# Clustered attention and a SoLU layer on one core: v rows 72 elements apart, contiguous key tiles, and every engine's order written anew

## The chip, the cores and the metric

The kernel runs on one core of one Trainium2 chip. The metric is the device time of one execution in microseconds (us), the median of several runs. TensorE (PE), VectorE (DVE), ScalarE (ACT), GpSimd (POOL) and SyncE (SP, which issues the transfers) each take their own instructions in order and wait for one another by semaphores.

## What is computed

Four batches, eight heads, 768 tokens, heads of 64. Queries and keys are each assigned to one of 16 clusters, a query attends to keys of its own cluster, and the result passes through a layer of width 1024 with a softmax-gated unit and a normalisation:

```
q_assign = argmax(q_n @ c_n);  k_assign = argmax(k_n @ c_n)
scores   = where(q_assign == k_assign, (q @ k.T) / 8, -1e9)
attn     = softmax(scores) @ v                    # 4 x 8 x 768 x 64
x        = attn, heads side by side               # 3072 x 512
h        = x @ w_in                               # 3072 x 1024
u        = h * softmax(h)
out      = ((u - mean(u)) / sqrt(var(u) + 1e-6) * g_ln) @ w_out
```

## The kernel before

**Pairs.** The work is cut into 16 pairs of heads (4 batches with 4 pairs), and the pairs' results into 24 blocks of 128 tokens for the layer (f = 0 to 23). For each pair the loads bring q and k as fp32 (tile `raw`). In batch 0 tokens lie on partitions and TensorE turns them (L387); in batches 1 to 3 the load (`load`, L397) puts blocks of 32 tokens by 32 columns, and DVE's 32x32 stream transpose (`turn`, L408, output `xt`) turns each block in place. Then `xt` is cast into the bf16 tile `qk` (L434, L436; ACT in batch 0, L432), rows 0 to 63. Four small matmuls on `xt` give the cluster scores (L446, L451, `csc`); DVE turns them back (L460, `cst`), takes the maximum (L473), makes one-hot rows (L479, L485), turns these (L492, L495, `oht`), and they are placed as 16 or 32 more rows under the heads in `qk` by DVE, POOL or, in four cases, an SP transfer (L507, L513, L515). With them the score matmul adds a large constant where query and key share a cluster, and the exponential takes it away again, so that no mask is needed.

**Attention.** `scores` (L602) multiplies a tile of 128 keys (the weights) with 128, 256 or 384 queries into one of three PSUM banks `sps`; ACT's exponential (L608) writes `e`; `values` (L625) takes 128x128 of `e` as the weights and a row of v as the moving operand, 64 columns and one column of ones for the denominators, six matmuls for each block of 128 queries, into `ops`, of which there is one bank. `normalise` (L637, L650) divides into `x`. In batches 1 to 3 the keys of tile kt are `slice(kt, S, n_t)`, every sixth column of `qk` from kt on, to fit v, which is loaded with six neighbouring tokens on one partition (`load_v`, L528; cast by L533 to `v1`). In batch 0 the keys of a tile are already neighbours in `qk`.

**The layer.** For block f: an SP transpose `xT` (L680), two matmul groups h into two of three banks `hreg` (L711), the row maximum (L717, `nmax`), the exponential (L723, `e_sb`), the product u (L730), statistics (L741, L745), an SP transpose `uT` (L735), matmuls y with the centred w_out (L775, `yps`), the scale (L751 to L760 on POOL for alpha; L790 on ACT or L792 on DVE) and the store (L802).

**What sets the order.** Every piece of work is an operation with a name (`S12.1` for a bank of scores, `V12.0` for six value matmuls, `h5.0.1`, `xt1.2.1`, `ld1.2.1.2`, `li0`). `Weave.ORDER` (L28) holds for each of the five engines a text of kinds and repeats, as `S2 V h`; `queues` (L108) takes the operations of a kind in turn. `AWAY` says which operations leave their usual engine. An operation's needs become semaphore waits. A transfer of SP also waits until the earlier one that used its completion semaphore has landed, so that only some transfers are in flight. Idle matmuls (`wm`, `fl`, L820) run on TensorE in the first 10 us, where it has nothing else to do.

Of the kernel before, what the change touches and what calls it, by code (L numbers as in the profile page):

```python
# [10 lines left out]
F32 = mybir.dt.float32  # L11
BF16 = mybir.dt.bfloat16
# [10 lines left out]
class Weave:  # L23
# [3 lines left out]

    ORDER = {}  # L28
    ORDER["SP"] = """
        ld4 lv si ld4 lv lg ld4 lv2 ld4 lo2 ld4 lo ld3 lo ld3 li4 tx ld3 lv3 tx ld4 tu ld9 lv ld tu  # L30
        tx ld3 tu ld3 ou ld2 ou ld tu ld12 tu ld4 lv ld2 ou tx ld3 tu ou ld2 tx lv ld tu ld4 tx ld
        tu ou2 ld lv ld4 tu ld4 tu ld ou ld7 pl ou ld lv2 ld3 tu lv tx ou tu lv pl ld4 ou2 tx lv tu
        tx ou tu pl2 tu2 tx tu tx ou2 tx ou tu tx2 ou tu2 ou2 tu2 ou6
    """
    ORDER["POOL"] = """
        po z ca2 pl2 cv z bl pl2 ca z ca pl2 ca z2 ca3 cv ca cv ca pl3 sg ca cv2 pl3 ca2 gs pl ca cv
        ca wi ca pl2 wi3 bl ca pl2 cv at cv pl ca pl al bl at cv ca pl ca pl cv ca3 al at ca al ca
        at ca pl2 bl cv pl2 ca4 at ca2 al ca pl2 bl pl2 cv2 ca3 al at pl2 bl pl2 ca pl al ca3 at cv
        at pl ca pl2 ca2 pl al cv2 bl cv2 pl2 ca pl al pl at al at pl2 ca3 at al bl cv pl2 bl cv2
        ca3 pl5 al cv3 at al ca2 cv ca cv ca2 at ca2 pl ca al pl2 at2 pl3 at ca cv al at2 al2 at2 al  # L40
        at al3 at al2 at2 al2
    """
    ORDER["PE"] = """
        wm tp fl3 cp fl2 tp2 cl tp fl10 cl fl8 S3 tp2 S2 tp S cq S tp S2 tp2 S2 V3 S cl S tp2 V3 S gt S tp S
        tp S2 cl S2 V2 S V S2 tp S2 tp S2 V2 S V S2 cl S2 V2 S V2 S3 V S2 V2 S2 V S cl S3 su S2 V3 S
        V S3 V3 S2 V S su S2 V S V3 S3 me S3 V4 S3 cl S3 V4 S2 h S h S2 h S h S2 V3 S2 V h S h V S V
        S h S V S V S h S2 V3 S2 V h S2 h V2 S y3 S2 h3 S3 y V3 h V S2 V2 S cl S3 h2 S2 V3 S y2 S V
        h2 S V y2 S h S V h S2 h S y3 S2 y V3 h S3 cl V2 S V S y S2 y2 S3 V3 S y S2 V3 S2 cl S V S2
        V2 S h S2 V2 S V S h S2 V2 cl V2 S3 y2 S V S2 V y S2 y V2 S3 h2 S V h S h S2 V h S V S V y2
        S h V y2 S2 V S h3 S cl V S2 V2 S h V cl S3 h2 V y V S3 y2 V S h V3 S y S h S2 h2 S3 V2 y h  # L50
        S V S2 y V3 y S3 h3 y S3 V3 S h S V S V cl S V S h S cl V2 S3 y V2 S y S2 y V2 S3 h y V S3 V
        h V2 S3 cl S2 V2 S y3 S2 y S V3 S V S y S2 V S V3 S2 y2 S3 y V2 S2 h V2 S3 h3 S V S2 V y S V
        h2 V2 S y S2 y V y S h2 S3 cl h V S2 V3 S h V2 S3 h2 S y S2 V h S2 V y2 V4 S3 y h S2 h V h V
        S V S y2 S3 V3 h2 S2 h2 S2 y2 S V S h2 S V3 S2 h S h S2 V S y V2 S V y2 S2 h2 S2 h2 V2 S2 V2
        y S2 h V2 h V S2 h S V h S3 V2 h y S V y3 V h3 S2 y3 S2 y h2 V2 h y h y3 h V h V y4 h ptx h
        y4 h2 y3 h2 y ptu2 y6 ptu y ptu y5
    """
    ORDER["DVE"] = """
        cn cb xa ca tb mx oh ot pl2 tb mx oh ot xa3 bl cf cv xa zo xa2 tb ca mx oh gk N ot tb pl mx
        xa2 oh xa cv N ot tb pl N xt mx xt N oh ot tb pl2 ca N pl xt mx N sk oh N ot xt ce3 N tb ce5  # L60
        N hm mx N u oh ot bn N bn ag hm xt2 u N bn2 hm ag sc xt u N bn tb hm mx bn oh ag u xt bn ot
        xt N cv hm bn ag sc xt tb mx N u xt oh ot sc N bn2 xt ag xt tb N hm mx tb N oh ot u xt mx N
        bn oh bn xt hm ot ag N cv u bn2 xt hm tb mx u N tb oh mx hm ot bn2 oh ag u N sc ag hm bn ot
        u bn N xt2 ag xt2 hm tb N bl mx tb bn2 oh u N xt ag xt sc hm ot tb mx oh N bn sc N u bn N ag
        xt ot bn ca N mx sc oh hm u bn ag N xt hm bn2 bl tb u ot ag N hm mx bn2 u bn N oh ot hm bl2
        u ag N cv hm sc bn u N hm ag bn N bn u bn2 hm ag2 N bn u bn2 N ag hm bn u N ag hm bn2 u bn2
        hm sc u N ag2 bn tx hm bn sc u bn ag hm bn tu ag u2 bn2 ag sc
    """
    ORDER["ACT"] = """
        wa xa2 ca2 xa ca2 E12 xa2 E6 xa E58 ex E12 ex E8 ex E8 ex E3 sc E5 ca E2 ex E25 ex E9 sc E6  # L70
        ex E5 sc E2 ex E9 ex E8 ex E9 sc E6 ex E18 ex E21 ex E5 sc E3 ex E9 ex E7 sc E2 ex E7 ex E8
        ex E7 ex E6 sc E ex E2 sc E3 ex E2 sc ex sc ex sc ex tu sc tu2 sc2 oz
    """
    AWAY = {}
    AWAY.update(dict.fromkeys("""
# [35 lines left out]
    def queues(self):  # L111

        of = {}
        for i, o in enumerate(self.ops):
            of.setdefault((o["eng"], o["kind"]), []).append(i)
        queues = {}
        for e, text in self.ORDER.items():
            queues[e] = []
            for kind, n in re.findall(r"([A-Za-z]+)(\d*)", text):
                for _ in range(int(n or 1)):  # L120
                    queues[e].append(of[e, kind].pop(0))
        assert not any(of.values()), {k: len(v) for k, v in of.items() if v}
        return queues
# [46 lines left out]
def kernel(  # L170
# [42 lines left out]
    mo = ctx.enter_context(tc.tile_pool(name="mo", bufs=2))  # L213
# [32 lines left out]
    SRC = (q, k)  # L246
# [35 lines left out]
    for b in range(B):  # L282
        for p in range(n_pair):
            a, c = 2 * p, 2 * p + 1
# [112 lines left out]
    def load(b, p, i, c, eng):  # L397
        if (b, p, i) not in raws:
            raws[b, p, i] = ld.tile([P, n_j, NB], F32, name="raw")
        eng.dma_start(  # L400
            out=raws[b, p, i][c * NB:(c + 1) * NB],
            in_=SRC[i][b, 2 * p + c // 2, :, (c % 2) * NB:(c % 2 + 1) * NB]
            .rearrange("(j i) c -> i j c", i=NB))
# [174 lines left out]

    def keep_sums(e):
        src = hreg[:, 1, :]  # L580
        uses(nc.scalar.copy(w_sum[:], src) if e == "ACT" else
             nc.vector.tensor_copy(w_sum[:], src), 1)

    def mean_w_out():
        uses(nc.tensor.matmul(hreg[:, 2, :], g_mean[:], w_sum[:]), 1, 2)

    def centre_w_out(fc):
        uses(nc.vector.scalar_tensor_tensor(out=w_out_c[:, fc, :], in0=w_g[:, fc, :],
# [6 lines left out]
    def scores(n, k):  # L595
        u = UNITS[n]
        b = u["b"]
        sps_[n, k] = ps_s.tile([P, 512], F32, name="sps", tag="sps")
        for h, kt, s0, w, c0 in u["banks"][k]:
            r = used(b, h)  # L600
            keys = slice(kt * P, (kt + 1) * P) if by_token(b) else slice(kt, S, n_t)
            nc.tensor.matmul(sps_[n, k][:, c0:c0 + w], side(b, h // 2, 1, h % 2, keys)[r],  # L602
                             side(b, h // 2, 0, h % 2, slice(s0 * P, s0 * P + w))[r])

# [234 lines left out]
    nc.gpsimd.memset(v1[0][:, :, :, D:], 1.0)  # L839

    c_n = const.tile([P, 2, D], F32, name="c_n")
    c_nsq = const.tile([P, 1], F32, name="c_nsq")
# [58 lines left out]
    for idx, (b, p) in enumerate(pairs):  # L901
        first = first_of(b, p)
        if by_token(b):
            for hf, i in ((hf, i) for hf in range(2) for i in range(2)):
                if not halves_of(b, p):
                    i, hf = hf, i
                t = f"{b}.{p}.{i}"
# [6 lines left out]
                e = "ACT" if (b, p) == (0, 0) and i == hf else "DVE"  # L914
# [5 lines left out]
        for i in range(2):  # L920
            t = f"{b}.{p}.{i}"
# [30 lines left out]
            for hh in range(2):  # L952
                for hf in range(2) if halves_of(b, p) else (None,):
# [3 lines left out]
                    e = "ACT" if hf is not None and i == 1 else "POOL"  # L957
# [5 lines left out]
        t = f"{b}.{p}"  # L963
# [297 lines left out]
```

## Time and profile before

| what | value |
|---|---|
| median of 3 runs | 226.29 us (224.62 to 227.29) |
| span of the profiled execution | 223.1 us, 3.2 us less than the median |
| instructions in the profile | 6642 |
| busy share of the span | PE 96%, DVE 88%, ACT 86%, POOL 57% |
| first score matmul | at 9.52 us |
| read from HBM, written to it | 23.11 MB, 6.29 MB |

The profile is one execution, from the first instruction to the last; the runs' times also hold what lies around it. An engine's busy time is the union of its instructions, and a matmul's end in it is modelled: matmuls overlap in the pipeline, so what a stream of them costs is read from the distance of their starts, not from their mean duration. Some matmul records can be missing. A row of a group names the line, the engine, the operation, output <- inputs, shapes and count, then busy us, mean ns of one, and the idle time of the engine before them.

### The profile page before, as it was taken

The numbers are of one execution on the slowest core, as the hardware profiler recorded it, in microseconds if no ns is written. First come the engines' busy times: TensorE is split into PE (matmuls) and PEld (weight loads), VectorE is DVE, ScalarE is ACT, GpSimd is POOL, SyncE is SP. The second block draws the span as 40 slices with busy tenths as digits, with TensorE's granted clock in tenths as the row PEclk, the third lists the DMA queues.
The fourth block names the chain that finished last, engine by engine and source line by source line (L and its number), as shares of the span: only waits on it lengthen the run. The fifth ranks groups of instructions, "written<-read, shape, count | busy, mean of one in ns | idle before, by whom it ended". The sixth has DMA issues, their size and how long they took to land.

```text
span 223.1 us, 6642 instructions
## 1 busy us (share of the span) xinstructions
PE 214.7 (96%) x2422; PEld 149.8 (67%) x2454; DVE 197.0 (88%) x359; ACT 192.1 (86%) x372; POOL 127.0 (57%) x247
## 2 busy tenths in 40 slices
PE   7899999999999999999999999999999999999994
PEld 6576656677566777776577667787677777755452
DVE  3799898999999989999998999887999889888982
ACT  3779999999888999998889899999999998983363
POOL 3499842774793999547668543944796403022331
PEclk9999999999999999999999999999999999999999
DMA  6999888989999998899999879199940528385923
GB/s 151 333 299 183 240 171 240 341 203 200 166 180 180 207 156 152 190 174 205 149 268 152 175 147 240 67 207 220 223 59 9 98 51 140 79 156 148 177 80 141
DMA packets 125679, 38.80 MB, mean 174 GB/s; under 512 B 115016, under 2 KB 121168, under 8 KB 125648
## 3 DMA queue, kind: packets, MB, share of 16 engines
q1 hardware_dynamic: 123904, 37.87, 82.3%
q10 hardware_dynamic: 1744, 0.52, 1.0%
q8 instruction: 19, 0.31, 0.6%
q14 instruction: 12, 0.10, 0.1%
HBM read 23.11 MB, written 6.29 MB: 132 GB/s over the span
## 4 chain that ended last, share of the span: by engine, by line
PE 83%; ACT 5%; DVE 4%; issue 3%; DMA 3%; SPq 1%; ACTq 0%; DVEq 0%
PE sps L602 27%; PE hreg L711 17%; PE yps L775 17%; PE ops L625 14%; ACT e L608 5%; PE csc L451 4%; DMA raw<-in_q_dram 2%; PE hreg L387 1%; DVE u L730 1%; DMA raw<-in_k_dram 1%; PE hreg L575 1%; PE hreg L775 1%; PE csc L446 1%; DVE bs L741 1%; DVE xt L408 0%
## 5 line engine op out<-in xcount | busy, mean ns | idle before, releaser
L608 ACT ACTIVATE e<-sps 128x512 bf16<-128x512 f32 (+1 forms) x294 | 151.1, 599 | 12.2 <-PE sps L602 10.2
L602 PE MATMUL sps<-qk 80*128 80x256 bf16 (+5 forms) x636 | 94.0, 264 | 1.4 <-ACT e L608 0.5
L602 PEld LDWEIGHTS <-qk 80*128 80x128 bf16 (+1 forms) x636 | 60.1, 121 | 27.6 <-issue 9.0
L625 PEld LDWEIGHTS <-e 128*128 128x128 bf16 x1152 | 50.4, 97 | 12.4 <-issue 1.9
L625 PE MATMUL ops<-v,e 128*128 128x65 bf16 x1152 | 55.0, 193 | 0.1
L711 PE MATMUL hreg<-w_in_sb,xT 128*128 128x512 bf16 x173 | 49.1, 379 | 1.3 <-DVE u L730 0.2
L775 PE MATMUL yps<-w_out_c,uT 128*128 128x512 bf16 x171 | 46.5, 379 | 0.6
L515 POOL COPY qk<-oht 32x384 f32<-32x384 f32 (+1 forms) x50 | 24.4, 487 | 15.8 <-DVE oht L495 13.2
L730 DVE TENSOR_TENSOR u<-e_sb,hreg 128x1024 bf16<-128x1024 bf16 (+1 forms) x25 | 29.1, 1168 | 4.7 <-ACT e_sb L723 4.5
L741 DVE BATCH_NORM_STATS2 bs<-u 128x6 f32<-128x512 bf16 x48 | 31.5, 677 | 0.1
L717 DVE TENSOR_REDUCE nmax<-hreg 128x1 f32<-128x1024 f32 x24 | 29.0, 1209 | 2.6 <-PE hreg L711 2.2
L723 ACT ACTIVATE e_sb<-hreg,nmax 128x1024 bf16<-128x1024 f32 x24 | 26.9, 1120 | 4.5 <-DVE nmax L717 4.4
L434 POOL CAST qk<-xt 64x768 bf16<-64x768 f32 (+1 forms) x31 | 26.0, 840 | 5.0 <-DVE xt L394 3.5
L775 PEld LDWEIGHTS <-uT 128*128 128x128 bf16 x200 | 18.2, 97 | 11.7 <-issue 0.3
L757 POOL TENSOR_SCALAR esq<-es,mv 128x1 f32<-128x1 f32 x24 | 8.5, 355 | 29.4 <-DVE mv L745 21.2
L436 POOL TENSOR_SCALAR qk<-xt 64x768 bf16<-64x768 f32 (+1 forms) x28 | 22.9, 820 | 1.7
L408 DVE STREAM_TRANSPOSE xt<-raw 128x768 f32<-128x768 f32 x24 | 22.8, 955 | 0.7 <-issue 0.5
L711 PEld LDWEIGHTS <-xT 128*128 128x128 bf16 x192 | 16.7, 97 | 9.8 <-DVE u L730 1.0
L751 POOL TENSOR_SCALAR es<-esum 128x1 f32<-128x1 f32 x24 | 5.3, 221 | 26.4 <-ACT e_sb L723 25.9
L650 DVE TENSOR_TENSOR x<-ops,den 128x256 bf16<-128x256 f32 (+1 forms) x39 | 19.0, 486 | 1.3
L760 POOL TENSOR_TENSOR alpha<-esq,halves 128x1 f32<-128x1 f32 x24 | 13.5, 561 | 2.0
L533 POOL CAST v<-vf 128x384 bf16<-128x384 f32 x27 | 13.6, 516 | 1.1 <-DMA vf<-in_v_dram 0.4
(80 smaller groups left out, 167.8 us busy)
## 6 DMA issues: line engine op xcount, KB each, us to landing
vf<-in_v_dram SPq DMA_DIRECT2D x16, 384.0 KB, 4.2
out_dram<-y SPq DMA_DIRECT2D x23, 256.0 KB, 2.6
raw<-in_q_dram SPq DMA_DIRECT2D x50, 96.0 KB, 3.4
raw<-in_k_dram SPq DMA_DIRECT2D x50, 96.0 KB, 3.0
w_g<-in_moe_w_out_dram SPq DMA_DIRECT2D x4, 512.0 KB, 5.8
w_st<-in_moe_w_in_dram SPq DMA_DIRECT2D x4, 512.0 KB, 5.2
raw<-in_q_dram SPq DMA_DIRECT2D x3, 384.0 KB, 6.6
raw<-in_k_dram SPq DMA_DIRECT2D x3, 384.0 KB, 7.2
```

The source lines that it names most:

```text
L434: VEC[e].tensor_copy(dst, src)
L436: VEC[e].tensor_scalar(dst, src, scalar1=inv_C, scalar2=1.0, op0=Alu.mult, op1=Alu.mult)
L515: ins = VEC[e].tensor_copy(dst.bitcast(F32), src.bitcast(F32).unsqueeze(1) .to_broadcast([NB, 2, n // 2]))
L602: nc.tensor.matmul(sps_[n, k][:, c0:c0 + w], side(b, h // 2, 1, h % 2, keys)[r], side(b, h // 2, 0, h % 2, slice(s0 * P, s0 * P + w))[r])
L608: nc.scalar.activation(es[n, k][:, :w], sps_[n, k][:, :w], Act.Exp, scale=exp_scale, bias=-exp_scale)
L625: nc.tensor.matmul(opss[g][:, s, :VW], es[n, k][:, c0:c0 + P], v1[slot(b, h // 2)][:, h % 2, kt, :VW], start=(kt == 0), stop=(kt == n_t - 1))
L711: uses(nc.tensor.matmul(hreg[:, at(f, f2)[1], :], xTs[f][:, dc, :], w_in_sb[:, dc, f2 * FF2:(f2 + 1) * FF2], start=(dc == 0), stop=(dc == ...
L717: uses(nc.vector.tensor_reduce(ff[f, "nmax"][:], pair_of(f), axis=AXY, op=Alu.max, negate=True), *both(f))
L723: uses(nc.scalar.activation(ff[f, "e"][:], pair_of(f), Act.Exp, bias=ff[f, "nmax"][:], accum_out=ff[f, "esum"][:]), *both(f))
L730: uses(nc.vector.tensor_tensor(ff[f, "u"][:, at_], ff[f, "e"][:, at_], pair_of(f)[:, at_], op=Alu.mult), *banks)
L741: nc.vector.bn_stats(ff[f, "bs"][:, f2, :], ff[f, "u"][:, f2, :])
L775: ins = nc.tensor.matmul(dst, ff[f, "uT"][:, at(f, f2)[0] * (n_fc // 2) + c, :], w_out_c[:, fc, cols], start=(fc == chunks[0]), stop=(fc = ...
```

## The change

**Rows of v.** The tile `v1` has 72 elements a row, where it had 66, of which 65 are read as before. The memsets of the column of ones write the same columns.

**Keys of batches 1 to 3.** The load of keys reads the tokens in another order: the column block j of `raw`, which held tokens 32 j to 32 j + 31, now holds for j = 4 t + g the 32 tokens 192 g + 6 i + t, i = 0 to 31. After the transpose and the casts the 128 keys of tile t lie side by side. Query loads stay.

**One tile less.** The sums of w_out's columns go into a buffer of `y` instead of `w_sum`.

**Order.** The text of each engine is another one. It may now also name an operation outright, with `=`, ahead of its turn. The operations of each engine are the same as before, but for the idle matmuls of TensorE: 33 `fl` for 23.

```
-            for kind, n in re.findall(r"([A-Za-z]+)(\d*)", text):
+            for word in text.split():
+                if word[0] == "=":
+                    i = self.by[word[1:]]
+                    of[e, self.ops[i]["kind"]].remove(i)
+                    queues[e].append(i)
+                    continue
+                kind, n = re.match(r"([A-Za-z]+)(\d*)$", word).groups()
...
     VS, VW = D + 2, D + 1
+    VR = 72
...
-    v1 = [big.tile([P, 2, n_t, VS], BF16, name=f"v1_{i}") for i in range(R)]
+    v1 = [big.tile([P, 2, n_t, VR], BF16, name=f"v1_{i}") for i in range(R)]
...
-        eng.dma_start(
-            out=raws[b, p, i][c * NB:(c + 1) * NB],
-            in_=SRC[i][b, 2 * p + c // 2, :, (c % 2) * NB:(c % 2 + 1) * NB]
-            .rearrange("(j i) c -> i j c", i=NB))
+        src = SRC[i][b, 2 * p + c // 2, :, (c % 2) * NB:(c % 2 + 1) * NB]
+        dst = raws[b, p, i][c * NB:(c + 1) * NB]
+        if i == 0:
+            eng.dma_start(out=dst, in_=src.rearrange("(j i) c -> i j c", i=NB))
+        else:
+            eng.dma_start(out=dst.rearrange("i (t g) c -> i t g c", t=n_t),
+                          in_=src.rearrange("(g i t) c -> i t g c", i=NB, t=n_t))
...
-    w_sum = const.tile([P, d_model], F32, name="w_sum")
...
-            keys = slice(kt * P, (kt + 1) * P) if by_token(b) else slice(kt, S, n_t)
+            keys = slice(kt * P, (kt + 1) * P)
...
     ORDER["SP"] = """
-        ld4 lv si ld4 lv lg ld4 lv2 ld4 lo2 ld4 lo ld3 lo ld3 li4 tx ld3 lv3 tx ld4 tu ld9 lv ld tu
+        li ld4 lv si ld5 lv lg ld lv lo ld3 lo ld5 lo2 ld li lv ld4 li2 tx ld5 lv ld tx ld2 lv ld2
```

In the built program the source of a key load in batches 1 to 3 has the counts 192x4x32 and the destination 32x24x32; before, both had 32x24x32. The compiler's input marks a transfer whose pattern was prepared at build time; the 48 key loads of batches 1 to 3 had that mark and no longer have it, and all other loads keep it.

Three places of the order. First SP's queue behind the five loads of the first pair: the loads of q and k of pairs 1 to 3 (`raw`), of v (`vf`) and of w_in (`w_st`). Before:

```order
L528 DMA vf_131<-in_v_dram 128x2x384
L375 DMA raw_196<-in_q_dram 128x2x384
L375 DMA raw_198<-in_k_dram 128x2x384
L375 DMA raw_207<-in_q_dram 128x2x384
L375 DMA raw_215<-in_k_dram 128x2x384
L528 DMA vf_217<-in_v_dram 128x2x384
```

After:

```order
L551 DMA vf_130<-in_v_dram 128x2x384
L572 DMA w_st_165<-in_moe_w_in_dram 128x1024
L394 DMA raw_198<-in_q_dram 128x2x384
L394 DMA raw_201<-in_k_dram 128x2x384
L394 DMA raw_208<-in_q_dram 128x2x384
L394 DMA raw_216<-in_k_dram 128x2x384
L394 DMA raw_223<-in_q_dram 128x2x384
L551 DMA vf_233<-in_v_dram 128x2x384
```

A first block of w_in stands ahead of all loads of pairs 1 to 3, and a third query load ahead of the second v load.

Second, DVE's queue where the placed rows of the first pair's first half are made (`oht`, then the copies into `qk0`), with the second half's cluster scores (`csc`, `cst`) behind. Before:

```order
L495 STREAM_TRANSPOSE oht_260<-oh_253 128x192
L515 COPY qk0_99<-oht_260 32x2x96 x2
L460 STREAM_TRANSPOSE cst_278<-csc_266 128x192
L473 TENSOR_REDUCE mx_285<-cst_278 128x12
L485 TENSOR_TENSOR oh_293<-cst_278,mx_285 128x192
```

After:

```order
L518 STREAM_TRANSPOSE oht_267<-oh_257 128x192
L483 STREAM_TRANSPOSE cst_282<-csc_273 128x192
L538 COPY qk0_99<-oht_267 32x2x96 x2
L496 TENSOR_REDUCE mx_299<-cst_282 128x12
L508 TENSOR_TENSOR oh_308<-cst_282,mx_299 128x192
```

The second half's transpose has moved ahead of the two copies.

Third, DVE's queue where the layer's blocks 1 and 2 begin and the third pair of batch 1 is transposed, its queries first, then its keys (two `xt`). Before:

```order
L717 TENSOR_REDUCE nmax_1347<-hreg_111 128x1
L408 STREAM_TRANSPOSE xt_1376<-raw_1006 128x768
L408 STREAM_TRANSPOSE xt_1406<-raw_1140 128x768
L730 TENSOR_TENSOR u_1422<-e_sb_1384,hreg_111 128x1024
L637 RECIPROCAL den_1442<-ops_1322 128x6
L650 TENSOR_TENSOR x_1441<-ops_1322,den_1442 128x6x64
L741 BN_STATS bs_1454<-u_1422 128x6 x2
L717 TENSOR_REDUCE nmax_1470<-hreg_111 128x1
```

After:

```order
L431 STREAM_TRANSPOSE xt_1379<-raw_1065 128x768
L753 TENSOR_TENSOR u_1393<-e_sb_1368,hreg_111 128x1024
L660 RECIPROCAL den_1425<-ops_1319 128x6
L673 TENSOR_TENSOR x_1424<-ops_1319,den_1425 128x6x64
L764 BN_STATS bs_1438<-u_1393 128x6
L764 BN_STATS bs_1357<-u_1244 128x6
L768 BN_AGGR mv_1467<-bs_1357 128x2
L740 TENSOR_REDUCE nmax_1469<-hreg_111 128x1
L431 STREAM_TRANSPOSE xt_1495<-raw_1154 128x768
```

The transpose of the keys, which stood ahead of u of block 1, stands behind the row maximum of block 2.

More of the change, by code (lines that the diff above doesn't have):

```diff
@@ new lines @@
+        cv2 wi3 =pl1.0.0.1 =pl1.0.1.1 ca cv =pl1.0.0.0 pl cv bl at ca2 pl3 cv =ca1.1.1.0 pl cv al bl
+        ca at al =ca1.2.1.1 ca =ca1.2.1.0 =pl1.2.1.1 =cv1.3.0 pl =pl1.2.0.1 ca pl =at3 ca cv bl
+        =ca1.3.1.0 at al =ca2.0.0.0 ca al =pl1.3.0.0 pl =ca2.0.0.1 =pl1.3.0.1 pl ca cv bl =cv2.1.1
+        =pl2.0.1.1 pl =ca2.1.0.0 at bl =ca2.0.1.1 pl al at ca pl =ca2.1.1.1 al =ca2.1.1.0 ca
+        =cv2.1.0 pl =ca2.2.1.0 =pl2.1.0.0 ca =pl2.1.0.1 cv =ca2.3.1.1 pl =ca2.2.1.1 bl at al
+        =ca2.3.0.1 =ca2.3.0.0 at2 =pl2.3.1.0 =cv2.3.1 cv =pl2.2.0.1 pl2 al =pl2.3.1.1 pl ca =cv2.3.0
@@ new lines @@
+        y S V S h V y V2 S2 V h cl S2 h S2 h S V y S y S2 V y V h V2 S y h S V S2 h S y h S V S y S
+        V S V y S2 V y V2 h S3 cl S V2 S V S V y S2 y S y S2 y S V2 S2 cl S V4 S V2 S2 cl S h S V h
+        S V S V2 S h S2 V S y2 S y S V3 y S2 h2 S2 h V2 h S2 V h S2 h V y S2 y2 S y S V S h2 S V cl
+        S3 h V2 S h V cl V S h S h S h S V S V S y2 S V2 y S y S2 h S V2 h S3 h V S V2 y S h y S V2
+        y V S h S2 y S V S V S h S V h S h S V cl V2 S2 h S2 cl V S V S y V2 S y S V S V y S2 h S y
@@ new lines @@
+        S V2 S h S cl S V S2 V3 S y S2 y S V2 y2 S V S V S y S y S V S V2 S V S2 y S V S y V S V h
+        S2 V S h S h S V S h S2 V S V h V h V S2 y3 S2 V y h S h V S V S2 h cl V h S2 V S V2 S y S h
+        S V S h V S2 h S y S V y V S2 y h S V2 S h2 S2 V2 S V h S V2 S h y S V S h S h V2 S2 h S2 V2
+        h y2 S y S h S h S V S2 V2 h V h S2 y V y S2 h2 S V S V2 S h y h V2 S y S2 V h V h y S y2 S
+        h V S V S h S y h S h y2 S V S V h S y h S y V h2 y V y3 h V h y4 V h2 y2 ptx y2 h2 y3 h2 y
@@ L57 @@
+        ptu2 y6 ptu2 y6
     """
     ORDER["DVE"] = """
[L59 to L63, printed above, removed]
@@ L580, in keep_sums @@
         src = hreg[:, 1, :]
-        uses(nc.scalar.copy(w_sum[:], src) if e == "ACT" else
-             nc.vector.tensor_copy(w_sum[:], src), 1)
+        wt["sum"] = mo.tile([P, d_model], F32, name="y")
+        uses(nc.scalar.copy(wt["sum"][:], src) if e == "ACT" else
+             nc.vector.tensor_copy(wt["sum"][:], src), 1)
     def mean_w_out():
-        uses(nc.tensor.matmul(hreg[:, 2, :], g_mean[:], w_sum[:]), 1, 2)
+        uses(nc.tensor.matmul(hreg[:, 2, :], g_mean[:], wt["sum"][:]), 1, 2)
     def centre_w_out(fc):
```

62 lines of the change are left out of this document (31 added, 31 removed).

## Prediction

> **What bounds the kernel now.** I read the page's busy times and its chain of work first, then the table by stage, then groups and single rows of the stages that matter.
>
> ```profile
> span 223.1 us, 6642 instructions
> ...
> PE 214.7 (96%) x2422; PEld 149.8 (67%) x2454; DVE 197.0 (88%) x359; ACT 192.1 (86%) x372; POOL 127.0 (57%) x247
> ...
> PE 83%; ACT 5%; DVE 4%; issue 3%; DMA 3%; SPq 1%; ACTq 0%; DVEq 0%
> ```
>
> The profiled execution spans 223.1 us; the median of the three runs is 226.29 us, so 3.2 us lie around the span, and I carry them over unchanged. TensorE is on 83% of the chain that ended last. How close the others are is told only by stage (us, then busy us and instructions of PE, PEld, DVE, ACT and POOL, then TensorE's granted clock, DMA's share, GB/s):
>
> ```profile
> 10.00:60.00 50.00, 48.67 (x604) 33.93 (x605) 45.82 (x90) 47.23 (x99) 34.10 (x61) 1.00 1.00 232
> 60.00:120.00 60.00, 59.37 (x661) 41.93 (x673) 57.87 (x99) 54.94 (x106) 43.16 (x76) 1.00 1.07 186
> 120.00:205.00 85.00, 84.04 (x988) 60.19 (x1004) 75.36 (x128) 77.35 (x147) 41.00 (x82) 1.00 0.66 134
> 205.00:224.00 19.00, 14.66 (x95) 7.71 (x93) 12.79 (x24) 7.66 (x14) 5.05 (x13) 0.95 0.49 125
> ```
>
> The clock is full until the tail. From 10 to 60 us no engine is alone the bound: PE 97%, ACT 94%, DVE 92%. From 60 to 205 us PE is busy 143.4 of 145 us: there a matmul that takes less time is worth its time, as long as DVE follows, which has 2.1 us left of 60 in the first part (96%) and 9.6 of 85 in the second. After 205 us there are almost no attention matmuls.
>
> **The change part by part.** First, the value matmuls (L625), whose moving operand is a row of v. Their rows of 65 columns stood 132 bytes apart and so began at 0, 4, 8 or 12 bytes past a multiple of 16; with 72 elements all begin on one. How much is there to gain? A busy time of a row runs to the modelled end of its last matmul; less one matmul's own duration it is the sum of the starts' distances:
>
> ```profile
> L625 PE MATMUL ops<-v,e 128*128 128x65 bf16 x1152 | 55.0, 193 | 0.1
> ...
> L711 PE MATMUL hreg<-w_in_sb,xT 128*128 128x512 bf16 x173 | 49.1, 379 | 1.3 <-DVE u L730 0.2
> ...
> L602 PE MATMUL sps<-qk 80*128 80x256 bf16 x288 | 47.7, 274 | 1.0 <-ACT e L608 0.5
> ...
> L699 PE MATMUL utp<-ident_b,u 128*128 128x128 bf16 x16 | 1.4, 219 | 0.0
> ...
> 66.27 1.03 PE L711 MATMUL hreg<-w_in_sb,xT 128*128 128x512 bf16 x4
> 67.13 0.60 PE L602 MATMUL sps<-qk 80*128 80x256 bf16 x4
> 67.57 0.73 PE L625 MATMUL ops<-v,e 128*128 128x65 bf16 x18
> ...
> 213.50 0.61 PE L699 MATMUL utp<-ident_b,u 128*128 128x128 bf16 x8
> ```
>
> 512 columns: (1030-379)/3 = 217 ns. 128 columns: (610-219)/7 = 56 ns. That is 0.419 ns a column and 2.3 ns fixed, so 65 columns should take 29.6 ns (an estimate from these rows). They take (730-193)/17 = 31.6 ns. The 2.0 ns between are what the rows' starts can cost; over 1152 matmuls 2.3 us. Bounds: 0 (the 2.0 ns belong to a short matmul, not to its address) and 2.3. I take the upper end, for the three longer shapes lie on the line within 1 to 2 ns and this one alone reads rows of mixed starts. Where they lie in time:
>
> ```profile
> 60.00:205.00 145.00, 39.76 (x822) 36.42 (x823) 1.00 0.83 156
> ```
>
> 822 of them lie where PE is the bound: 1.6 us. Of the other 330, nearly all before 60 us (0.65 us), I count half, since ACT and PE alternate there: 0.3. Term: -1.9 us.
>
> Second, keys. In batches 1 to 3 the score matmul's weights were taken with a step of 6 elements; now they are contiguous, as in batch 0 already. The weight load itself shows it, 10 to 40 us (mostly batch 0) against 60 to 200 us:
>
> ```profile
> L602 PEld LDWEIGHTS <-qk 80*128 80x128 bf16 x79 | 6.4, 97 | 6.1 <-issue 4.1 <-ACT e L608 0.9 <-POOL qk L507 0.6
> ...
> L602 PEld LDWEIGHTS <-qk 80*128 80x128 bf16 x234 | 23.5, 127 | 8.4 <-ACT e L608 0.6 <-issue 0.6
> L602 PEld LDWEIGHTS <-qk 96*128 96x128 bf16 x240 | 23.5, 127 | 7.8 <-issue 1.9
> ```
>
> 30 ns less for each of 474 loads would be 14 us if they were exposed. They are not: four strided score matmuls stand (600-274)/3 = 109 ns apart, where the line asks 110. So the load hides behind the matmul before it, except perhaps where that one is a short value matmul: the 32-ns matmuls cannot cover 127 ns. Bounds: 0, and about 60 such places times 30 ns = 1.8 us; I take 0.5, nearer the measured spacing. The Trainium skill, "SBUF — State Buffer", Door 1 (the note on cachelines), says that consecutive accesses to one 16-byte line run at full rate and each crossing costs: by that the load with a step of 12 bytes is slow, and the trace agrees, 127 against 97 ns. By the same note a 130-byte row touches nine lines from any of the four starts, so the value matmuls would gain nothing, and the sum would be 1.9 us smaller; that is the third rival below, priced there from rows.
>
> Third, the order. Every engine issues the same set of work as before, only in another order; TensorE alone gets ten more idle matmuls in its first 10 us, set where it waits (56 ns each, hidden by the wait for the first placed rows). Three places carry a price.
> (a) DVE at 55 us. The chain runs through a key load that came late:
>
> ```profile
> 55.29 2.11 DMA raw<-in_k_dram
> 57.40 0.49 issue
> 57.89 0.98 DVE xt L408
> 58.87 1.12 DVE u L730
> 60.03 1.47 PE hreg L711 x6
> ```
>
> The transpose xt of that load is now behind u, a normalisation, statistics and the next nmax, so u and the following matmuls of hreg no longer wait for the load. DVE loses 0.5 us of idle; between 0 and 2.6 us (2.11 + 0.49) go, I take 0.6, since PE had other work for most of it. Next late there is the pair's own score matmul, several us further on.
> (b) The start. The first block of w_in (512 KB) goes out ahead of all loads of pairs 1 to 3; in slice 2 the queues moved 333 GB/s, so those land some 1.5 us later. And DVE does the second half's transpose (0.38) before the two copies that the first scores wait for:
>
> ```profile
> GB/s 151 333 299 183 240 171 240 341 203 200 166 180 180 207 156 152 190 174 205 149 268 152 175 147 240 67 207 220 223 59 9 98 51 140 79 156 148 177 80 141
> ...
> 8.89 0.57 DVE L515 COPY qk<-oht 32x192 f32<-32x192 f32 x2
> ...
> 9.49 0.38 DVE L460 STREAM_TRANSPOSE cst<-csc 128x192 f32<-128x192 f32 x1
> 9.52 0.79 PE L602 MATMUL sps<-qk 80*128 80x384 bf16 x3 [0.35 <-DVE qk L515]
> ```
>
> The first scores begin 0.4 us later, and the second half's rows 0.6 us earlier. Between -0.5 and +1.5; I take +0.3.
> (c) Bursts. In many places three or four matmul pairs of hreg or yps that stood together now alternate with scores. ACT waited 10.2 us for scores in all; from 60 us on it is not the bound, so that is worth nothing there. From 10 to 60 us it was idle 2.8 of 50 us: between 0 and 2.8, I take 0.5.
>
> Fourth, what costs more. The key loads' patterns no longer have the same counts on both sides (192x4x32 in HBM, 32x24x32 in SBUF), and the built program no longer marks these 48 as prepared at build time. In the kernel before only the four copies of placed rows by SP (L513) lack that mark. Their issue beside those of marked transfers:
>
> ```profile
> 148.59 0.63 SPq L513 DMA_DIRECT2D qk<-oht  x1
> ...
> 205.10 0.33 SPq L802 DMA_DIRECT2D out_dram<-y  x1
> ...
> 49.92 2.84 SPq L400 DMA_DIRECT2D raw<-in_k_dram  x3
> ...
> 58.27 2.16 SPq L400 DMA_DIRECT2D raw<-in_k_dram  x4
> ```
>
> A key load took 0.54 us; unmarked it takes between 0.63 (+0.09) and 0.54+0.30 (+0.30): 4 to 14 us more of SP over 48 loads. SP is hardly free there, but part of it is waiting inside the instruction (three loads took 2.84 where 1.6 would do), and a later start only shortens such waits. Behind a key load in SP's queue stand query loads, v loads and the transposes xT and uT, for which hreg and yps wait. I take 0, cover: SP's own waits and the buffers loaded ahead; the other end is the first rival. The casts of v write rows 144 instead of 132 bytes apart, the same count: 0.
>
> Sum: -1.9 -0.5 -0.6 +0.3 -0.5 = -3.2 us. Span 219.9, time 226.3 - 3.2 = 223.1 us; 221 to 225 if each term takes half or all of its reach.
>
> **The rivals.** First, on the other side: SP becomes late. Place: 15 to 120 us, where some 40 of the key loads are issued and DMA stands at a share of about 1.0. It decides once a load costs more than SP's waits give back; at +0.3 us each 40 loads are 12 us, and if half of that reaches xt and uT, the time is 226.3 + 6 - 3.2 = 229.1 us. For it: one load already arrived too late at 55 us. Against it: that xt has been moved back.
> Second, DVE takes the bound: it was busy 57.9 of 60 us from 60 to 120, so there at most about 1 us can go, and if the tighter order adds a few waits on normalisations (PE waits for the one bank of ops), the gains of 60 to 120 us and of (c) vanish, and what is left is the value and key terms of 120 to 205 us, about 1.2 us: 226.3 - 1.2 = 225.1 us. For it: 96%. Against it: DVE's slack of 9.6 us in the next stage.
> Third, the rows' start makes no difference to a value matmul, the 2.0 ns being what a short matmul with a weight load of its own costs: 226.3 - 1.3 = 225.0 us. For it: no row here shows an aligned 65-column matmul apart. Against it: the longer shapes have a weight load of their own too, and lie on the line. The Trainium skill's note on cachelines, above, counts in its favour.
> Fourth, the order brings more than I see: all of the idle time of (c), 2.3 us more, and all of (a), 2.0 more: 226.3 - 3.2 - 2.3 - 2.0 = 218.8 us.
>
> **How the numbers follow.** My forecast 223.1 (221 to 225) has 0.56, rival one 0.14, two 0.13, three 0.10, four 0.07. About 1%, 2.3 us, is what a measurement of this kernel tells from no change: faster by over 1% means below 224.0. Of the forecast's 0.56 some 0.46 lie there, with rival four 0.53. Rivals two and three and the forecast's upper part are within 1%, 0.33, with 0.02 of rival one's small end, 0.35. Slower: 0.12. The range 219.5 to 227.5 leaves out most of rivals one and four, 0.18.
>
> **What would show it.** Eighteen value matmuls should take (x - 193)/17 = 29.6 ns; the weight loads L602's line should all be at 97 ns; PE's busy time should fall by about 2.5 us while its idle time from 60 to 205 us stays near 1.6 us. In the chain no load should stand near 55 us. Four key loads in SP's row should not exceed 3.4 us, and xt should not wait for a DMA. The prediction is wrong if xt or hreg wait for transfers, if PE waits for DVE from 60 to 120 us, or if a value matmul still takes 31.6 ns.

## The result, and the profile after

The changed kernel is slower: 234.99 us median of 4 runs (232.06 to 237.31) against 226.75 us, ratio 1.0281 with the interval 1.0210 to 1.0351; two of the four executions (237.31 and 237.20 us) were granted 0.993 of TensorE's clock on average and two (232.06 and 232.78 us) 1.0, and the ratio takes the latter two alone. I had forecast 223.1 us. The page after is of the 237.31 us execution; before had PE 96% and 83% of the chain:

```profile
span 235.0 us, 6685 instructions
...
PE 218.9 (93%) x2464; PEld 143.4 (61%) x2464; DVE 200.6 (85%) x359; ACT 193.9 (83%) x372; POOL 128.3 (55%) x247
...
PE 47%; DVE 18%; DMA 17%; POOL 8%; SPq 5%; issue 4%; ACT 1%; POOLq 0%; DVEq 0%; ACTq 0%
```

But for ten idle matmuls no engine got more work (weight loads went from 2454 to 2464; the profile before lacks 32 matmul records). Every share fell, and half of the chain is now something other than TensorE. TensorE's granted clock in this trace is 0.83 from 10 to 20 us, so the places of the loss are read below from the new order run by itself, whose trace has 1.00 there and still 70% of the chain on TensorE. The local effects came nearly as predicted. Value matmuls, score weight loads, and the key loads on SP after, the last against before:

```profile
L648 PE MATMUL ops<-v,e 128*128 128x65 bf16 x1152 | 57.6, 193 | 1.6 <-DVE v L556 0.9 <-DVE x L673 0.5 <-POOL qk L538 0.2
L625 PEld LDWEIGHTS <-qk 80*128 80x128 bf16 x372 | 30.3, 97 | 27.2 <-issue 6.7 <-POOL qk L530 2.7 <-POOL qk L538 2.6
```

```profile
L425 SPq DMA_DIRECT2D raw<-in_k_dram x48: 590/658/2659, 21.3 to 157.9; - x48
```

```profile
L400 SPq DMA_DIRECT2D raw<-in_k_dram x48: 430/535/2376, 17.0 to 151.3; - x48
```

All score weights load in 97 ns (127 before), and a key load takes SP 658 ns in the median instead of 535 (the three numbers behind the colon are minimum, median and maximum in ns). The busy time of the value matmuls is no measure of their distance here: the new order has them in 138 bursts instead of 113, and each burst counts the modelled end of its last matmul. What PE waited for tells more. Us in all, times and longest, after and then before:

```profile
PE csc L474 <- DVE y L815: 2.4, 2, 1.3
PE yps L798 <- DMA uT<-u: 2.2, 1, 2.2
PE sps L625 <- POOL qk L530: 1.4, 2, 1.1
PE hreg L406 <- DMA raw<-in_q_dram: 1.2, 1, 1.2
PE sps L625 <- POOL qk L538: 1.1, 2, 0.8
PE idle_p L843 <- DVE halves L847: 1.0, 1, 1.0
PE ops L648 <- DVE v L556: 0.9, 1, 0.9
```

```profile
PE idle_p L820 <- DVE halves L824: 1.0, 1, 1.0
PE sps L602 <- ACT e L608: 0.5, 2, 0.3
PE sps L602 <- DVE qk L515: 0.3, 1, 0.3
PE cps L865 <- DVE c_n L856: 0.3, 1, 0.3
PE hreg L387 <- DMA raw<-in_q_dram: 0.3, 1, 0.3
PE hreg L711 <- DVE u L730: 0.2, 1, 0.2
```

Before, the waits of PE other than the idle matmuls' sum to 1.6 us, none above 0.5. After, there are five above 1 us, on four resources: a scale y of DVE, a transfer uT, rows placed by GpSimd (twice), a first load. Of these the wait for uT is largely this execution's own: in the trace of the new order alone PE waits for it 0.5 us.

### The profile page after: what moved, and what is told of

Read it like the earlier page. It is cut to its first block, busy times and chain, and to the rows that moved or that the text cites. A ratio compares the mean times of both kernels' runs of the same rounds, so it can differ in the third digit from the quotient of the medians.

```text
span 235.0 us, 6685 instructions
## 1 busy us (share of the span) xinstructions
PE 218.9 (93%) x2464; PEld 143.4 (61%) x2464; DVE 200.6 (85%) x359; ACT 193.9 (83%) x372; POOL 128.3 (55%) x247
## 4 chain that ended last, share of the span: by engine, by line
PE 47%; DVE 18%; DMA 17%; POOL 8%; SPq 5%; issue 4%; ACT 1%; POOLq 0%; DVEq 0%; ACTq 0%
PE sps L625 13%; PE yps L798 12%; PE hreg L734 10%; PE ops L648 7%; DMA raw<-in_k_dram 6%; DMA raw<-in_q_dram 4%; DMA vf<-in_v_dram 4%; DMA uT<-u 3%; SPq L425 3%; DVE u L753 3%; DVE bs L764 2%; PE csc L474 2%; DVE nmax L740 2%; PE hreg L406 2%; POOL qk L459 2%
## 5 line engine op out<-in xcount | busy, mean ns | idle before, releaser
L625 PE MATMUL sps<-qk 80*128 80x256 bf16 (+5 forms) x636 | 101.0, 263 | 3.4 <-POOL qk L530 1.4
L625 PEld LDWEIGHTS <-qk 80*128 80x128 bf16 (+1 forms) x636 | 51.5, 98 | 39.8 <-issue 8.1
L648 PEld LDWEIGHTS <-e 128*128 128x128 bf16 x1152 | 52.1, 97 | 15.5 <-issue 3.5
L648 PE MATMUL ops<-v,e 128*128 128x65 bf16 x1152 | 57.6, 193 | 1.6 <-DVE v L556 0.9
L734 PE MATMUL hreg<-w_in_sb,xT 128*128 128x512 bf16 x192 | 55.9, 379 | 0.1
L798 PE MATMUL yps<-w_out_c,uT 128*128 128x512 bf16 x184 | 50.7, 379 | 2.2 <-DMA uT<-u 2.2
L457 POOL CAST qk<-xt 64x768 bf16<-64x768 f32 (+1 forms) x31 | 25.1, 810 | 6.8 <-DVE xt L413 2.2
L556 POOL CAST v<-vf 128x384 bf16<-128x384 f32 x27 | 14.2, 532 | 22.6 <-DMA vf<-in_v_dram 14.1
L813 ACT ACTIVATE y<-yps,alpha 128x512 f32<-128x512 f32 x13 | 9.0, 696 | 7.4 <-PE yps L798 4.4
```

The source lines that it names most:

```text
L457: VEC[e].tensor_copy(dst, src)
L648: nc.tensor.matmul(opss[g][:, s, :VW], es[n, k][:, c0:c0 + P], v1[slot(b, h // 2)][:, h % 2, kt, :VW], start=(kt == 0), stop=(kt == n_t - 1))
L734: uses(nc.tensor.matmul(hreg[:, at(f, f2)[1], :], xTs[f][:, dc, :], w_in_sb[:, dc, f2 * FF2:(f2 + 1) * FF2], start=(dc == 0), stop=(dc == ...
L798: ins = nc.tensor.matmul(dst, ff[f, "uT"][:, at(f, f2)[0] * (n_fc // 2) + c, :], w_out_c[:, fc, cols], start=(fc == chunks[0]), stop=(fc = ...
```

## The experiments

**Data or order.** Theory A: the written order made the loss. Theory B: the key loads, slower on SP since they are no longer prepared at build time, made it (my first rival). Four kernels take the change apart. The first has the new rows in the order of before:

```
+    VR = 72
-    v1 = [big.tile([P, 2, n_t, VS], BF16, name=f"v1_{i}") for i in range(R)]
+    v1 = [big.tile([P, 2, n_t, VR], BF16, name=f"v1_{i}") for i in range(R)]
-    w_sum = const.tile([P, d_model], F32, name="w_sum")
```

> The old order and the old key loads, with rows of v 72 elements apart and the w_out sums in a buffer of y. Theory A (the written order made the loss) and theory B (the unmarked key loads, slower on SP, made it) agree here: a value matmul falls from 31.6 to about 29.6-30.4 ns, and with 822 of them where TensorE is the bound the time falls by 1 to 2 us, to 225 us. If the old order has no room for it (each bank of ops is waited for by DVE just as long), it stays within 0.5 us of before.

225.31 us against 225.68, ratio 0.9962 (0.9926 to 0.9998): 0.9 us gained by the ratio, 0.4 by the medians. Eighteen value matmuls:

```profile
64.36 0.71 PE L626 MATMUL ops<-v,e 128*128 128x65 bf16 x18
```

(710-193)/17 = 30.4 ns, where they took 31.6. This is a mean of two kinds: in the trace of this run the median distance between 60 and 200 us is 29 ns, and about one in six is 35; before, the median was 32. The second has the new key loads and contiguous key tiles in the order of before:

```
-            .rearrange("(j i) c -> i j c", i=NB))
+            eng.dma_start(out=dst.rearrange("i (t g) c -> i t g c", t=n_t),
+                          in_=src.rearrange("(g i t) c -> i t g c", i=NB, t=n_t))
-            keys = slice(kt * P, (kt + 1) * P) if by_token(b) else slice(kt, S, n_t)
+            keys = slice(kt * P, (kt + 1) * P)
```

> The old order and the old rows of v, with the new key loads (contiguous key tiles). Theory A: the weight loads fall from 127 to 97 ns and are hidden, SP has cover in the old order, so within 1 us of before, 226 to 227 us. Theory B: 48 loads of 0.66 instead of 0.54 us on SP are 5.5 us of SP's time in a row, of which half or more reaches xT, uT and the loads behind: 229 to 231 us.

Ratio 1.0039 (1.0007 to 1.0070), 0.9 us lost (0.2 to 1.6), with the loads as slow on SP as in the changed kernel:

```profile
L406 SPq DMA_DIRECT2D raw<-in_k_dram x48: 590/659/2566, 18.1 to 152.8; - x48
```

The third has both of these edits and the order of before.

> Both changes of data, in the old order. Theory A: 224.5 to 226 us, a little below before. Theory B: most of the loss is here without the new order: 229 to 232 us.

Ratio 0.9992 (0.9954 to 1.0031): no loss. In its trace the slower loads do cost one wait, at the place of my term (a): the transpose xt that waits for a key load starts at 59.2 us (57.9 before), and u stands behind it. PE's wait and the chain there:

```profile
PE hreg L716 <- DVE u L735: 1.4, 1, 1.4
```

```profile
59.22 0.98 DVE xt L413
60.20 1.12 DVE u L735
...
61.36 0.82 PE hreg L716 x3
```

The fourth has the new order with the data of before.

```
-    VR = 72
+    VR = VS
-            keys = slice(kt * P, (kt + 1) * P)
+            keys = slice(kt * P, (kt + 1) * P) if by_token(b) else slice(kt, S, n_t)
```

> The new order alone: old rows of v, old marked key loads, keys taken with a step of six. Theory A: the loss stays, 232 to 235 us, with the waits of raw, vf and uT still in the chain. Theory B: key loads back at 0.54 us, the loss goes, 225 to 228 us. If it takes both (an order with tight leads and loads that are slow to issue), it lies between, about 229 us.

232.45 us, ratio 1.0279 (1.0225 to 1.0334): the whole loss. Theory B falls: with the old loads the new order loses as much as with the new ones (1.0279 and 1.0281). By stage, with the columns of the first table of the prediction:

```profile
10.00:60.00 50.00, 45.69 (x572) 30.96 (x573) 42.50 (x82) 44.68 (x92) 31.23 (x52) 1.00 0.91 212
60.00:120.00 60.00, 57.86 (x635) 40.54 (x644) 56.13 (x96) 54.88 (x104) 41.22 (x74) 1.00 1.07 180
120.00:205.00 85.00, 83.45 (x986) 60.30 (x999) 76.48 (x130) 77.47 (x149) 46.29 (x89) 1.00 0.68 135
```

PE is idle 4.3 us from 10 to 60 (1.3 before) and 2.1 from 60 to 120 (0.6): the loss begins at the start, where I had seen no bound. Its waits in this run:

```profile
PE sps L621 <- POOL qk L526: 1.9, 2, 1.1
PE csc L470 <- DVE y L811: 1.5, 2, 1.3
...
PE hreg L406 <- DMA raw<-in_q_dram: 0.8, 1, 0.8
```

All of PE's waits listed for this trace, without the idle matmuls', sum to 6.4 us where before had 1.6, which is 4.8 of the 6.3 us; the three rows above are 4.2 of the 6.4. Two of them lead to GpSimd's queue. The chain from 27 us on, up to a score matmul, and that from 76 us on, up to cluster scores:

```profile
27.03 0.82 POOL qk L453
27.85 0.91 POOL qk L455
...
28.88 1.05 POOL w_in_sb L571
...
29.98 0.92 POOL qk L526
...
31.14 0.51 POOL qk L526
...
31.69 0.83 PE sps L621 x6
```

```profile
76.63 0.51 POOL v L552
...
77.19 0.50 POOL qk L534
...
82.00 0.83 POOL qk L455
82.83 0.19 POOL es L770
...
83.54 0.58 POOL alpha L779
84.14 0.76 DVE y L811
84.94 0.85 PE csc L470 x8
```

The reader is to see the order of the work, not its length. At 27 us GpSimd casts queries or keys (L453, L455) and a block of w_in (L571) first, and places the rows (L526) that the scores wait for after that. At 76 us ten operations, the first of them a cast of v before which GpSimd itself stood idle for 1.4 us, stand ahead of es and alpha of block 2; DVE's scale y waits for alpha, and `csc` waits for y, since both use one PSUM bank.

**Each suspect alone, in the order of before.** Here one place differs from the order of before (and the sums of w_out's columns are in a buffer of `y`, as in the changed kernel). `li0` is the first block of w_in; `ca` casts q or k, `pl` places rows, `at` and `al` are es and alpha of a block.

```
SP:
- si ld0.1.0 ld0.1.1 ...
+ si li0 ld0.1.0 ld0.1.1 ...
```

> The order of before with one transfer moved: the first block of w_in ahead of the loads of pairs 1 to 3, as in the new order. My prediction took +0.3 us for it, between -0.5 and +1.5. If the late loads reach the end (first load of pair 1 landing at 11.2 instead of 9.6 us, PE idle 0.8 us at 11 us), 227 to 227.5 us, 1.004 to 1.007; if ACT, which is the bound at 16 to 30 us there, covers it, 225.8 us, 1.000.

Ratio 1.0068 (1.0040 to 1.0097): 1.5 us lost, with this wait:

```profile
PE hreg L513 <- DMA raw<-in_q_dram: 0.8, 1, 0.8
```

```
GpSimd:
- cv0.3.0 pl0.2.1.0 pl0.2.0.0 pl0.2.0.1 ca0.3.0.1 ca0.3.1.0 gs pl0.3.1.1 ca0.3.1.1
+ cv0.3.0 ca0.3.0.1 ca0.3.1.0 ca0.3.1.1 pl0.2.0.0 pl0.2.1.0 pl0.2.0.1 gs pl0.3.1.1
```

> The order of before with the copies of pair 2's placed rows on GpSimd behind three casts of the next pair (some 2.5 us), about as in the new order. If GpSimd's place for these rows makes a loss of the start by itself, PE waits 0.5 to 1.5 us for them at 28 to 31 us and the time rises by as much: 226.3 to 227.3 us, 1.002 to 1.007; if the scores in hand cover it, 225.8 us, 1.000.

Ratio 1.0070 (1.0037 to 1.0102): 1.6 us lost. PE waits 1.3 us, in the chain:

```profile
26.88 0.83 POOL qk L562
...
27.75 0.50 POOL qk L633
...
28.84 0.61 PE sps L728 x4
```

```
GpSimd:
- al1 at2 ca1.2.1.0 al2 ca1.2.1.1 at3 ca1.3.0.0 pl1.2.1.0 ... ca1.3.0.1 ca1.3.1.0 ca2.0.0.0
+ al1 ca1.2.1.0 ca1.2.1.1 at3 ca1.3.0.0 pl1.2.1.0 ... ca1.3.0.1 ca1.3.1.0 at2 al2 ca2.0.0.0
```

> The mirror on the kernel before: its order, with es and alpha of block 2 put behind eleven casts and copies on GpSimd, about where the new order has them. If that place makes the loss, DVE's scale of block 2 waits some 5 us or more, csc and u of block 4 behind it, and the time rises by 1.3 us or more: 227.5 to 231 us, 1.006 to 1.02. If there is enough cover, 226 us, 1.000.

Ratio 1.0141 (1.0099 to 1.0184): 3.2 us lost by two operations of 1.1 us, set 11 places later. The chain shows the three engines in a row:

```profile
79.06 0.58 POOL alpha L886
...
79.66 0.76 DVE y L918
...
80.47 0.85 PE csc L577 x8
```

PE's wait at this place:

```profile
PE csc L577 <- DVE y L918: 2.2, 1, 2.2
```

Part of the price is not the wait but TensorE's clock behind it. In the columns of the stage tables, where the third number from the end is the granted clock:

```profile
78.00:80.00 2.00, 0.30 (x3) 0.04 (x1) 0.34 (x1) 1.86 (x5) 1.81 (x5) 1.00 0.49 77
...
82.00:84.00 2.00, 2.00 (x14) 1.19 (x13) 1.79 (x4) 1.19 (x2) 1.73 (x4) 0.50 0.96 154
```

From 81.5 us the clock is 0.5 for 3.4 us, which costs 1.7 us; the wait of 2.2 and these make 3.9, and at its end this trace is 3.7 us behind that of before. Five more traces (the changed kernel, one mixture, and three with other moves) have such stretches of 3.4 us at 0.5 ahead of the tail, each beginning within 1.7 us of the end of an idle gap of PE of 1.2 to 2.6 us. Other gaps brought none (1.3 us in the trace with the rows late, 2.2 us at 164.5 us in the changed kernel), and what decides it is not shown.

The three moves cost 0.68, 0.70 and 1.41%, 2.8% in sum, as much as the whole new order. That the sums agree is chance: five of the six executions with alpha late were granted 0.992 or 0.993 of the clock, six of the ten with the rows late 0.985 to 0.992, while the new order alone had 0.999 or more in all six. By the medians of executions with 0.996 or more the three cost 1.0 us (10 executions), 0.5 (4) and 2.7 (one alone), 4.2 of the 6.8 us that the new order costs by the same measure. What is lost stays lost. Starts of the exponential with this number in the four traces (us):

| number | before | w_in first | rows late | alpha late |
|---|---|---|---|---|
| 105 | 70.24 | 71.13 | 71.14 | 70.17 |
| 150 | 98.85 | 99.73 | 99.86 | 102.61 |
| 285 | 192.06 | 192.94 | 193.14 | 195.81 |

From the place of the wait to the end the distance to before keeps to within 0.2 us; that of alpha late holds the 1.7 us of clock.

**Repairs inside the new order.** The same places the other way round: one in the changed kernel, three in the new order alone.

```
SP:                                          (changed kernel)
- li0 ld0.0.0.0 ... lv0.2 lo0
+ ld0.0.0.0 ... lv0.2 li0 lo0
```

> The changed kernel with one transfer moved: the first block of w_in (512 KB) goes out behind the loads of pairs 1 to 3 and the third load of v. If that block alone delays the start, the first load of pair 1 lands at 9.6 instead of 11.2 us, the second load of v some 2 us earlier, and 1 to 2 us of the end are given back: 230.5 to 231.5 us. If GpSimd's own order from 21 to 32 us is what counts, it waits no less there and the time stays at 232 to 232.5 us.

Ratio 1.0360 (1.0301 to 1.0418): nothing gained. The first load was on time, but other waits grew (uT 1.9 us, once, against 0.5 in the new order alone).

```
GpSimd:                                      (new order alone)
- ca1.2.1.0 pl1.2.1.1 cv1.3.0 pl1.2.1.0 ... bl1.2 ca1.3.1.0 at2 al2
+ ca1.2.1.0 at2 al2 pl1.2.1.1 cv1.3.0 pl1.2.1.0 ... bl1.2 ca1.3.1.0
```

> The new order alone (old rows, old key loads; 1.028 of before), with two GpSimd operations of block 2 (es, then alpha) put back ahead of the rows of the third pair of batch 1, as in before, instead of behind 13 casts and copies. If it is GpSimd's queue there that makes the second loss, PE's idle 1.26 us at 84.9 us (csc waits for DVE's scale y, which waits for alpha) goes, and with it 1 to 3 us of the end: 229.5 to 231.5 us, 1.015 to 1.024. If csc is then late for another reason, 232.5 us, 1.028.

Ratio 1.0235 (1.0175 to 1.0295), 1 us less than 1.0279, inside the interval.

```
GpSimd:                                      (new order alone)
- gs ca0.2.1.1 pl0.1.1.0 ... ca0.3.1.1 z3 wi0 pl0.2.0.0 z2 pl0.2.1.0
+ pl0.1.1.0 gs ca0.2.1.1 ... pl0.2.0.0 pl0.2.1.0 ca0.3.1.1 z3 wi0 z2
```

> The new order alone, with three copies of placed rows of batch 0 ahead on GpSimd: one of pair 1 ahead of the spread of g, two of pair 2 ahead of the next pair's casts and of the cast of w_in. If GpSimd's queue is the bound at 20 to 32 us, PE's two waits for these rows (0.86 at 23.5 and 1.07 us at 31.7) go: 230.5 to 231.5 us, 1.020 to 1.024. If what is gained at the start is lost again later, as when the first block of w_in was moved, the time stays at 232 to 232.5 us, 1.027.

Ratio 1.0259 (1.0215 to 1.0303): hardly anything. The wait for rows went, and the next one stood behind it, for a cast of v on DVE:

```profile
PE csc L577 <- DVE y L918: 1.5, 2, 1.3
PE ops L751 <- DVE v L659: 1.1, 1, 1.1
```

All three repairs together:

> The new order alone with these two repairs on GpSimd and the first block of w_in behind the loads of pairs 1 to 3. PE's idle time from 10 us on was 6.0 us against 0.9 before; the repairs aim at 0.8 + 0.9 + 1.1 + 1.3 = 4.0 of it. If PE's idle time is the loss, 228 to 229.5 us, 1.010 to 1.017. If the losses have another base (DVE's pace), 231 to 232.5 us.

Ratio 1.0174 (1.0131 to 1.0216), 230.30 us: 1.05 of the 2.8% come back. PE's waits still sum to 3.7 us in this trace, the largest 1.1 for that cast of v, 0.7 for a transfer uT and 0.6 for rows placed by DVE. Two further moves on DVE, one of them against that new wait:

```
DVE:                                         (new order alone, with the three repairs)
- N0 tb0.2 ca0.1.1.0 mx0.2 pl0.1.0.0 ... xt1.0.1 N3 pl0.3.1.0 cv0.2.0
+ N0 pl0.1.0.0 ca0.1.1.0 tb0.2 mx0.2 ... cv0.2.0 xt1.0.1 N3 pl0.3.1.0
```

> The new order alone with the two GpSimd repairs, the first block of w_in moved back, and two more repairs on DVE: the cast of v of pair 2 ahead of a transpose xt and two copies of rows (PE waited 1.09 us for it at 34.7), the rows of pair 1 ahead of the next pair's transposes and maximum (0.60 us at 22.4). If the start's loss is such a chain of single waits, 228.5 to 229.5 us, 1.010 to 1.013; if each wait removed only uncovers the next, 230 us, 1.017.

Ratio 1.0222 (1.0178 to 1.0265): no better, if not worse. My expectation that the start is a chain of single waits which can be taken out one by one fell.

**A suspect that was none.** In the changed kernel three key loads stood on SP behind the first xT, which waited for x:

```
SP:
- li2 li3 tx0 ld1.1.1.1 ld1.1.1.2 ld1.1.1 ld1.2.0.0
+ li2 li3 ld1.1.1.1 ld1.1.1.2 ld1.1.1 tx0 ld1.2.0.0
```

> The changed kernel with three key loads of the second pair of batch 1 ahead of the first transpose xT on SP, behind which they stood while it waited some 6 to 11 us for x. If that wait makes the second half of the loss (a transpose xt that comes 10 us late and drags the casts), the time falls by 1 to 3 us, to 230 us. If those keys are not needed before 60 us, nothing changes: 232 to 232.5 us.

Ratio 1.0354 (1.0282 to 1.0425): nothing gained. So those keys, issued some 14 us later than before, were not what counted.

**Where the rest lies.** Mixtures: the work up to a time in one order, the rest in the other.

```
-    queues[e] = new[e]
+    queues[e] = [x for x in old[e] if x in early] + [x for x in new[e] if x not in early]
```

> The changed kernel, but on every engine the work up to about 33 us (44 banks of scores, all of batch 0's loads, the first two pairs of batch 1) in the order of before, and the rest in the new order. Theory A1 (about 4 of the 6.5 us are lost at the start, where the late first loads make GpSimd the bound): 228 to 229 us. Theory A2 (the loss is spread over the whole order, by its tighter distances): 231 to 232 us.

> The mirror: the new order up to about 33 us (37 banks of scores), the order of before behind it. Theory A1: 229 to 230 us. Theory A2: 226 to 227 us. If the two halves only lose where they meet, both mixtures are above 230 us.

1.0358 (1.0291 to 1.0426) and 1.0076 (1.0032 to 1.0120). The first says nothing on the places: the orders don't fit at the cut, as PE's waits between 30 and 60 us show.

```profile
PE hreg L704 <- DMA w_g<-in_moe_w_out_dram: 2.0, 1, 2.0
PE hreg L841 <- DMA xT<-x: 1.2, 1, 1.2
```

The second puts about 0.8% on the start, if its cut costs nothing. The same cut at 105 us, with the repaired new order:

> The new order with the two GpSimd repairs and w_in moved back up to about 105 us (152 banks of scores), the order of before behind it. What the repaired new order still loses (1.017) is split by this and the next run. By the times of the exponentials 3.3 of the 5.2 us are lost by then: 229 us, 1.014, if the loss lies ahead of 105 us; 227 us, 1.006, if it lies behind. It means little if the two orders do not fit together at the cut.

> The mirror: the order of before up to about 105 us (157 banks), the repaired new order behind it. 227.5 us, 1.007, if the tail of the new order loses the other 2 us; 226 us, 1.000, if all was lost at the start; above 1.017 only if the cut itself costs.

1.0176 (1.0129 to 1.0222) and 1.0108 (1.0062 to 1.0154). They add up to more than the 1.0174 of the repaired order, so the losses of the two parts are not independent, or the cuts cost. It stays open where all of the remaining 1.7% lie: the 3.7 us of waits in the repaired order's trace, 2.1 more than before, cover about half. How much of the 2.8% the three moves make inside the new order is known only roughly: their waits are 4.2 of 6.4 us there, and repairing them gave back 2.4 us.

**Term (a) by itself**, on the third kernel (both data changes, old order):

```
DVE:
- xt1.2.0 xt1.2.1 u1 N11 bn1.0 bn1.1
+ xt1.2.0 u1 N11 bn1.0 xt1.2.1 bn1.1
```

> The changed data (rows 72 apart, contiguous key tiles with their slower loads) in the order of before, with one operation moved on DVE: the transpose xt of the keys of the third pair of batch 1 behind u of block 1, as in the new order. In that order with the changed data (0.999) PE waits 1.39 us at 61.4 for u, which stands behind an xt whose load landed at 59.1 (57.4 before). If my term for this move was right in kind, that wait goes: 225 us, 0.994 to 0.996. If the pair's score matmul is then late by as much, 0.999.

Ratio 1.0019 (0.9981 to 1.0057). The wait of 1.4 us for u is gone from PE's waits there, but against 0.9992 (0.9954 to 1.0031) no gain can be told. The trace does not say why: it is of an execution with a wait of 2.6 us for a transfer xT at 97.7 us and half the clock behind it. Of all versions the first, rows of v alone, is the fastest: 0.9962.

## Why the prediction was wrong

| step | predicted us | measured us (ratio - 1, times 225.7) |
|---|---|---|
| rows of v | -1.9 | -0.9 (e1) |
| contiguous keys, and their loads "I take 0" | -0.5 + 0 | +0.9 (e2) |
| the order: (a), (b), (c) | -0.6 + 0.3 - 0.5 | +6.3 (e4) |

**The step that failed is the third, "Three places carry a price".** Its terms sum to -0.8 us, and the order measured +6.3. I priced DVE's and SP's moves and the mix on PE, and never laid GpSimd's two queues side by side: its busy share (57% of the span, 34.1 of 50 us from 10 to 60) had put it out of question. But what counts of an engine that works in order is which operation stands ahead of the one waited for. One alpha 11 places later cost 3.2 us (in its trace 2.2 us of PE's wait and 1.7 us of clock behind it), rows behind three casts 1.6 us (1.3 us of wait in the trace); neither move was in my list, and no rival of mine had the order cost more than it gains. Two of my signs of being wrong came: hreg waited for a transfer, and PE for DVE between 60 and 120 us.

**(b) was mis-sized.** I took +0.3 us between -0.5 and +1.5; its SP half, the block of w_in ahead, alone costs 1.5 us (1.0 with the full clock), near the upper end; its DVE half was not run alone. The loads were late by as much as I said (pair 1's first at 11.0 us in the trace of that run, 9.6 before), but I let ACT and PE cover it, and at 11 us PE had nothing else: it waited 0.8 us at once.

**(c) had no basis.** I counted 2.8 us of ACT's idle time as room, and did not ask what a tighter order does to work that had been waiting in no one's way: PE's idle time from 10 to 120 us went from 1.96 to 6.45 us. The Trainium skill, "Perfetto Trace Analysis", Optimization Strategy, says to look for the gaps on the engine that should be saturated and for what blocks it there; by that rule the kernel before had 1.6 us of waits to give, and the runs agree as far as they go: none gained over 0.9 us.

**(a) was right in kind:** with the transpose behind u the wait for u goes. But before, PE waited only 0.2 us for that u, so my 0.6 was more than the place held.

**The rows of v** gave 1.2 of the 2.0 ns (31.6 to 30.4), 1.4 us over 1152 matmuls, of which 0.9 reached the end by the ratio. The mechanism was right, the size half. The Trainium skill's note on cachelines ("SBUF — State Buffer", Door 1), by which the starts should make no difference, is not borne out. My line through the longer shapes (29.6 ns) holds for most of them (median 29 ns), but not for the one in six that takes 35.

**The keys.** Their weight loads fell to 97 ns and stayed hidden, as said, with no gain at all. "I take 0" for the loads was wrong by about a microsecond in the order of before: 123 ns more for each, inside my bounds of 90 to 300. In the trace with both data changes they reach PE at 61 us; the trace of the loads alone has no such wait, and where its 0.9 us go is not shown. That is the first rival's mechanism at a seventh of what the order made; its number, 229.1 us, came nearest, for another reason, which is luck.

**The 3.2 us around the span** were a misreading that did no harm: the executions of the kernel before that give both take 1.9 or 2.0 us more than their span (224.43 and 222.5 us, for one), so the profiled execution was a faster one than the median. The forecast took its gain from the median.

## What to carry to other kernels

Where one engine is busy 97% or more, an order can gain only its idle time but can lose several times that, and a wait once made in the good order stayed to the end. An idle gap of 1.2 us or more on TensorE may also be followed by a stretch at half the clock, so read the granted clock behind each long wait before you price it. Compare the queue of every engine, the slack ones first, and for each operation that moved ask what is put ahead of it and who waits for it; a low busy share is no cover on an engine that works in order. When an edit and a new order come together, run the order alone and the data alone, and test a suspect by putting it into the good order, where nothing hides it: inside the bad one most repairs uncovered the next wait.

## What the runs showed of the hardware

The issue of a load on SP took 535 ns in the median with equal counts on both sides and 658 ns where source and destination had different ones (192x4x32 and 32x24x32) and the mark of preparation at build time was gone, with the minimum up from 430 to 590 ns; which of the two does it was not tried. Value matmuls of 65 columns came 30.4 ns apart when every row of v starts on a multiple of 16 bytes, and 31.6 ns when they start on 0, 4, 8 or 12. TensorE's granted clock fell to 0.5 for 3.4 us at a time near idle gaps of 1.2 to 2.6 us, in six of the twenty traces ahead of the tail; other gaps of 1.3 to 2.2 us brought no fall.
